# One pace for the weight slabs of a fused attention and gated-FFN layer, with its engine order planned anew

## The chip, the cores and the metric

One core of a Trainium2 chip runs the whole layer. The metric is the device time of one execution in microseconds, as the median of several. Below, PE is TensorE (matmul), ACT is ScalarE, DVE is VectorE, POOL is GpSimd and SP is SyncE, which here issues the DMA transfers.

## The reference

A pre-norm transformer layer over 2048 tokens with model width 1024: 32 query heads of 32 channels that share one key and one value head, then a feed-forward block of width 3584 whose gate is a sigmoid. All tensors are bf16.

```python
def _A_ref(x, wq, wk, wv, wo):
    q = (x @ wq).reshape(B, S, H, Dh).transpose(0, 2, 1, 3)
    k = x @ wk
    v = x @ wv
    p = softmax(einsum("bhqd,bkd->bhqk", q, k) * Dh ** -0.5)
    o = einsum("bhqk,bkd->bhqd", p, v)
    return o.transpose(0, 2, 1, 3).reshape(B, S, H * Dh) @ wo

def _B_ref(x, w_gate, w_up, w_down):
    g = einsum("bsd,df->bsf", x, w_gate)
    u = einsum("bsd,df->bsf", x, w_up)
    return einsum("bsf,fd->bsd", sigmoid(g) * u, w_down)

h = A_x + _A_ref(layernorm(A_x), A_wq, A_wk, A_wv, A_wo)
out = h + _B_ref(layernorm(h), B_w_gate, B_w_up, B_w_down)
```

## The kernel before

**The work.** Tokens are cut into 16 tiles of 128. A tile's attention has two halves of 16 heads each (32 halves in all), and a half is visited once for each of 16 key tiles: 512 visits. A visit is one score group, four matmuls of 512 columns on a quarter of the array's rows each (`S_ps<-QTb,kT`, emitted by `emit_S`), and two exponentials of 128x1024 on ScalarE (L707), which write the probabilities to one of ten slots `Pr` (at first also to four borrowed buffers). VectorE adds the probabilities up (`acc`, L680), so that row sums come from a short matmul over a selector (`F_ps<-acc,sel`, `mk_SUM`); for half 0 they come from matmuls with ones. `mk_PV` multiplies probabilities and values, `mk_OP` is the output projection of a tile (`F_ps<-wo_sb,OT`), `mk_GU` the gate and up matmuls with one tanh for each of 7 groups of 512 channels (L989; the sigmoid is made of a tanh), `mk_D` the down projection (`F_ps<-zone,hact`, 28 matmuls of 512 columns for each half of the width).

**From scores to the next stage.** After the row sums a reciprocal goes through memory to be spread over partitions (`r_scratch`, `rb`, L748 to L751), then OT is scaled (L765), projected, normalized (L871 and the statistics at L349 to L370), and transposed by DMA to `hnT` (`load_hT`), which the gate and up matmuls read.

**Two forms of gate and up.** Mostly the activations are the stationary operand and a weight slab streams, in matmuls of 512 columns (`F_ps<-ring,hnT`); the product then goes through a DMA transpose to `hact`. For the first `ws0` and the last `ws1` tiles the weights are stationary and matmuls of 128 columns give the transposed product at once (`F_ps<-hnT,ring`, four times as many).

**Weight slabs.** Gate and up weights are loaded anew for each tile in slabs of 1024x512, four quarters of 256 KB each (`load_next`), into a ring of four slabs. Once no scores are left, the slots `Pr` hold slabs as well. The two last groups of a pass are the first two of the next, so 40 quarters are loaded a pass. Transfers of slabs and of the down weights are paced: each is held back to the time at which the one before would be through at so many bytes a ns, by a wait on a ScalarE instruction that ends about then (`Plan.step`).

**The order of the work.** Nothing is scheduled on the chip. A planner (`Plan`, and the loop at the end of the kernel) lays out the instruction streams of all engines when the program is built, with costs for each instruction and an expected landing for each transfer. For PE it emits a score group when its inputs are known and ScalarE has less than `run` ns of exponentials in hand, and otherwise a matmul of the current group of another class, chosen by priority lists. Due times place the down groups among the gate and up groups. Copies out of PSUM go to ScalarE or VectorE, whichever the plan finds free first (`evac`), with a handicap for ScalarE of `eb` (keys, values and transposed x) or `eq` (queries). VectorE's additions are held back around the end of a PE group (`hold`). All these are numbers in `TUNE`, so that a change of any of them gives a new order on every engine.

The lines on which the pace hangs:

```python
def fast(self, s):
    return s < 200000.0 or s > self.t_last          # t_last: the plan's time of the last score group
...
if o.pace:
    self.pace_free = s + o.nbytes / TUNE["pace0" if self.fast(s) else "pace"]
```

Of the kernel before, what the change touches and what calls it, by code (L numbers as in the profile page):

```python
# [12 lines left out]
P = 128  # L13
# [2 lines left out]
SEM = 75.0  # L16


TUNE = dict(early=240, look=500, ln_v=1, warm=70, late=300, ws0=1, ws1=1, parts0=3, parts1=4, lord=2, h_ord=2,
            ho=3, ho2=0, pvl1=0, pvl2=0, col_ok=0, pace0=310, swait=400, parts=2, raw=1, rl=0, nd=2, pc=16,  # L20
            rate=315, pace=265, xd=4, qf=1, dall=1, wo_late=1, nkn=3, few=0, rmin=900, hmin=1, h0=100, h1=250,
            hf=1.35, run=700, sum_few=0, pv_few=4, d_off=0, d_a=-1, d_b=1, eb=450, eq=1500)


class Op:
# [16 lines left out]
class Plan:  # L42
# [48 lines left out]

    def fast(self, s):

        return s < 200000.0 or s > self.t_last

    def start_of(self, o):

# [3 lines left out]
        if o.eng == "dve" and o.prio >= 6:  # L101

            for p in self.heap["dve"]:
                if p.prio < 6 and s < p.ready < s + TUNE["look"]:
                    return p.ready
        return s

    def step(self, limit):
# [21 lines left out]
        if o.nbytes:  # L130
            if o.pace:
                self.pace_free = s + o.nbytes / TUNE["pace0" if self.fast(s) else "pace"]
            k = o.key.rstrip("0123456789_")
            go = max(s + 1720.0, self.dma_free)
            w = self.SLOW.get(k, 1.0) if k != "ha" else 2.5 if o.nbytes < 200000 else 1.3
            self.dma_free = go + o.nbytes * w / TUNE["rate"]
            o.end = self.dma_free + 700.0 + self.LATE.get(k, 0.0) + TUNE["late"]
        else:
# [31 lines left out]
def bass_sequential_preLN__grouped_kv_mqa__glu_gated_glu__prompt_kernel(  # L170
# [31 lines left out]
    with ExitStack() as es:  # L202
# [3 lines left out]
        def SB(name, shape, dt=BF16):  # L206
            return EC(nc.sbuf_tensor(name, [P] + shape, dt))
# [12 lines left out]
        r_sb = SB("r_sb", [64], F32)  # L220
# [18 lines left out]
        r_dram = nc.dram_tensor("r_scratch", [32, 64], F32, kind="Internal").ap()  # L239
# [30 lines left out]
        PE, ACT, DVE, POOL, SP = nc.tensor, nc.scalar, nc.vector, nc.gpsimd, nc.sync  # L270

        def dma(fn, key, nbytes, deps=(), prio=5, pace=False, order=(), occ=450.0):
            return pl.op("sp", fn, deps, occ=occ, key=key, nbytes=nbytes, prio=prio, pace=pace, order=order)
# [41 lines left out]

        for c in ["xxqxxqxxxxxxqxxxxq", "qxqxxqxqxxxxxxxxxx", "xqxqxqqxxxxxxxxxxx", "xqxqxqxqxxxxxxxxxx", "xxqxqxqxqxxxxxxxxx"][TUNE["lord"]]:
            if c == "x":
# [19 lines left out]
        def stats(ph, tiles, srcs, deps, prio, after=((), ())):  # L337
# [8 lines left out]
            for t, src, dp in zip(tiles, srcs, deps):  # L346
# [14 lines left out]
                      occ=90, lat=250)  # L361
            if ph and TUNE["ln_v"] or not ph and t0 < 2:

# [80 lines left out]
        def mm(o, l, r, start, stop, **kw):  # L444
            return lambda: PE.matmul(o, lhsT=l, rhs=r, start=start, stop=stop, **kw)  # L445
# [216 lines left out]
        RAW = tuple(range(TUNE["raw"])) + ((NH - 1,) if TUNE["rl"] else ())  # L662
# [20 lines left out]
        def flush_adds(hf):  # L683
            for kt in late_adds.pop(hf, []):
                make_add(hf, kt)
# [42 lines left out]
        rb_ld = {}  # L728
        rs_ev = {}
        rd_ld = {}  # L730
# [3 lines left out]
        def in_row(few):  # L734
            return v_done[0] >= NV or pl.pe_mode == "row" or len(free_slots) <= few or TUNE["col_ok"] and pl.pe_mode == "col"

        def mk_SUM(hf):
            a = acc[:, hf % 2, :]

            def atoms(b):  # L740
                return [(mm(F_ps[DH * j:DH * (j + 1), b, 0:64], sel[:, bb, :], a[:, j * 512 + bb * 64:j * 512 + (bb + 1) * 64],
                            bb == 0, bb == 7, tile_position=(0, DH * j)), 64, "col" if j == 3 else "col-", [])
                        for bb in range(8) for j in range(4)]

            def after(b, last):
                sum_last[hf] = last
                flush_adds(hf + 2)
                rc = pl.op("dve", lambda: DVE.reciprocal(r_sb[:, :], F_ps[:, b, 0:64]),  # L748
                           [last, rd_ld.get(hf - 1)], prio=0, occ=480, lat=560 + SEM)
                rd_ld[hf] = dma(lambda: SP.dma_start(r_dram, r_sb[0:P:4, :]), "rd", 8192, [rc] + (rb_ld[hf - 1] if hf - 1 not in RAW else []), prio=0)  # L750
                rb_ld[hf] = [dma(lambda j=j: SP.dma_start(  # L751
                    rb[DH * j:DH * (j + 1), :], bass.AP(r_dram.tensor, r_dram.offset + 512 * j, [[0, DH], [1, 512]])),
                    "rb", 65536, [rd_ld[hf], ot_ev.get(hf - 1), ot_ev.get(0)], prio=0) for j in range(4)]
                finish(hf)
                return [rc]
            return Group("SUM", atoms, lambda: [add_op.get((hf, NT - 1)), c_sel], after, lambda: in_row(TUNE["sum_few"]))

        def finish(hf):

            if hf not in rb_ld or (hf, len(parts_of(hf)) - 2) not in oun_ev:  # L760
                return
            c, hh = hf // 2, hf % 2
            o = oun[:, hf % 2, :]
            r = rs_b if hf == 1 and hf in RAW else rb[:, :]
            ot_ev[hf] = pl.op("dve", lambda: DVE.tensor_tensor(  # L765
                out=OT[:, 4 * hh:4 * hh + 4, :], in0=o.rearrange("p (a b) -> p a b", a=4),
                in1=r.rearrange("p (a b) -> p a b", a=4), op=ALU.mult),
                [oun_ev[(hf, len(parts_of(hf)) - 2)], op_last.get(c - 1)] + rb_ld[hf], prio=0, occ=600, lat=690)
            if hh == 1:
                for dc in range(2):  # L770
                    queues["OP"].append(mk_OP(c, dc))
# [326 lines left out]
        while True:  # L1098
# [15 lines left out]
            if v < NV:  # L1114
                run = max(pl.free["act"], t) + sum(o.occ for o in pl.heap["act"])
# [187 lines left out]
```

The softmax here doesn't subtract the row's maximum and nothing guards it: scores larger than these inputs give would overflow.

## Time and profile before

The time is 1092.22 us, the median of 3 runs (1091.94 to 1092.35). The profiled execution spans 1092.9 us at a granted PE clock of 0.998.

| engine | busy us | share of the span | instructions |
|---|---|---|---|
| PE, matmul | 1060.6 | 97% | 9314 |
| PE, weight load | 439.3 | 40% | 9454 |
| DVE | 848.9 | 78% | 1054 |
| ACT | 1000.7 | 92% | 1152 |
| POOL | 39.5 | 4% | 61 |

| stretch, us | PE busy | ACT busy | DMA share | GB/s |
|---|---|---|---|---|
| 0 to 50 | 44.05 | 35.48 | 0.83 | 204 |
| 100 to 200 | 96.40 | 98.75 | 0.74 | 227 |
| 500 to 600 | 97.96 | 100.00 | 0.80 | 231 |
| 1000 to 1020 | 19.73 | 10.48 | 1.01 | 299 |
| 1040 to 1060 | 19.32 | 2.39 | 1.04 | 295 |

The page's busy times are averages over three stages with different limits: a start in which the first queries, keys and values are made, a long middle in which scores run, and an end without scores. Matmuls overlap in the array, so a PE that is 97% busy isn't at its peak. In the page's groups of instructions a row gives the line and engine, the output and its inputs, shapes, the number of instructions, their busy time in all, the mean ns of one, and the idle time ahead of them with what ended most of it.

### The profile page before, as it was taken

What the parts mean: (1) busy time and instruction counts of PE and PEld (TensorE: products, weight loads), DVE (VectorE), ACT (ScalarE), POOL (GpSimd) and SP (SyncE); (2) the same over time, 40 slices, a digit from 0 to 9 for tenths busy, and PEclk for the clock granted to TensorE, in tenths of its full rate; (3) what the DMA queues carried; (4) which work ended last, traced back from release to release, by engine and by line L of the source; (5) the groups of instructions that cost most, each with busy time, mean ns of one, the idle gap of its engine ahead of it and who ended that gap; (6) DMA issues with size and microseconds to landing.
All of it is one profiled execution on the core that took longest, in us unless ns stands there. A gap on an engine that the chain in (4) does not pass through costs nothing.

```text
span 1092.9 us, 23470 instructions
## 1 busy us (share of the span) xinstructions
PE 1060.6 (97%) x9314; PEld 439.3 (40%) x9454; DVE 848.9 (78%) x1054; ACT 1000.7 (92%) x1152; POOL 39.5 (4%) x61
## 2 busy tenths in 40 slices
PE   8999999999999999999999999999999999999998
PEld 6533465333333333333333333333333333333485
DVE  8989988787887878787887878787887878787311
ACT  4999999999999999999999999999999999999010
POOL 3300000000000000000000000000000000000000
PEclk9999999999999999999999999999999999999999
DMA  8893399868769595868858595877858586876992
GB/s 248 171 306 121 116 300 279 251 170 269 203 182 266 137 271 144 246 183 255 231 166 256 139 270 147 260 189 229 245 150 262 138 250 168 248 206 194 287 307 95
DMA packets 296509, 233.70 MB, mean 214 GB/s; under 512 B 99536, under 2 KB 282832, under 8 KB 296400
## 3 DMA queue, kind: packets, MB, share of 16 engines
q1 hardware_dynamic: 296400, 232.19, 74.1%
q8 instruction: 75, 1.23, 0.5%
q14 instruction: 34, 0.28, 0.1%
HBM read 203.82 MB, written 8.12 MB: 194 GB/s over the span
## 4 chain that ended last, share of the span: by engine, by line
ACT 67%; PE 22%; issue 5%; DVE 3%; DMA 2%; SPq 0%; DVEq 0%
ACT Pr L707 62%; PE F_ps L445 19%; ACT tnh L989 5%; PE S_ps L445 3%; DVE acc L680 1%; DMA hnT<-hn 1%; DMA r_scratch<-r_sb 1%; DMA zone<-ring 0%; DVE st L349 0%; DVE st L351 0%; DMA ring<-in_A_x_dram 0%; DMA rb<-r_scratch 0%; DVE hact L285 0%; DVE ring L393 0%; DVE OT L765 0%
## 5 line engine op out<-in xcount | busy, mean ns | idle before, releaser
L707 ACT ACTIVATE Pr<-S_ps 128x1024 bf16<-128x1024 f32 x1008 | 956.1, 1181 | 3.4 <-PE S_ps L445 3.4
L680 DVE TENSOR_TENSOR acc<-acc,Pr 128x2048 bf16<-128x2048 bf16 x431 | 524.7, 1217 | 45.4 <-ACT Pr L707 32.1
L445 PE MATMUL F_ps<-ring,hnT 128*128 128x512 bf16 x1506 | 366.8, 380 | 4.4 <-issue 4.1
L445 PE MATMUL F_ps<-zone,hact 128*128 128x512 bf16 x813 | 212.1, 381 | 6.5 <-issue 4.3
L445 PE MATMUL S_ps<-QTb,kT 32*128 32x512 bf16 x2048 | 206.8, 385 | 5.6 <-ACT Pr L707 4.7
L445 PEld LDWEIGHTS F_ps<-ring,hnT 128*128 128x128 bf16 x1536 | 134.6, 98 | 180.8 <-issue 43.0
L989 ACT ACTIVATE tnh<-F_ps 128x512 f32<-128x512 f32 x112 | 83.7, 747 | 60.3 <-PE F_ps L445 60.3
L445 PEld LDWEIGHTS S_ps<-QTb,kT 32*128 32x128 bf16 x2048 | 53.7, 91 | 205.0 <-ACT Pr L707 123.9
L445 PE MATMUL F_ps<-Pr,Vt 128*32 128x512 bf16 x2016 | 134.1, 382 | 0.0
L445 PEld LDWEIGHTS F_ps<-zone,hact 128*128 128x128 bf16 x896 | 75.5, 97 | 104.0 <-issue 34.6
L1010 DVE SCALAR_TENSOR_TENSOR act_s<-tnh,F_ps 128x512 bf16<-128x512 f32 x98 | 67.2, 686 | 58.4 <-PE F_ps L445 58.3
L445 PE MATMUL F_ps<-zone 128*128 128x512 bf16 (+3 forms) x573 | 72.9, 272 | 4.3 <-DVE ring L393 1.0
L445 PEld LDWEIGHTS F_ps<-Pr,Vt 128*32 128x32 bf16 x2016 | 43.0, 95 | 68.0 <-issue 28.6
L445 PE MATMUL F_ps<-wo_sb,OT 128*128 128x512 bf16 x241 | 62.3, 381 | 2.5 <-issue 1.7
L367 POOL TENSOR_TENSOR dsb<-zb,cst 128x1 bf16<-128x1 bf16 x18 | 23.0, 1280 | 964.6 <-DVE zb L364 964.6
L1057 DVE SCALAR_TENSOR_TENSOR h_sb<-F_ps,h_sb 128x512 bf16<-128x512 f32 x32 | 22.1, 692 | 40.4 <-PE F_ps L445 40.3
L445 PEld LDWEIGHTS F_ps<-zone 128*128 128x128 bf16 x584 | 39.0, 97 | 31.3 <-issue 9.2
L680 DVE TENSOR_TENSOR acc<-Pr 128x2048 bf16<-128x2048 bf16 x31 | 37.9, 1224 | 9.7 <-ACT Pr L707 9.7
L445 PE MATMUL F_ps<-hnT,ring 128*128 128x128 bf16 x576 | 37.7, 223 | 0.7 <-ACT tnh L989 0.7
L807 DVE TENSOR_TENSOR oun<-F_ps,oun 128x512 f32<-128x512 f32 x34 | 23.4, 688 | 18.9 <-PE F_ps L445 18.8
L445 PEld LDWEIGHTS F_ps<-hnT,ring 128*128 128x128 bf16 x576 | 33.6, 100 | 6.7 <-issue 5.9
L445 PEld LDWEIGHTS F_ps<-wo_sb,OT 128*128 128x128 bf16 x256 | 21.3, 97 | 34.0 <-issue 12.5
(81 smaller groups left out, 350.9 us busy)
## 6 DMA issues: line engine op xcount, KB each, us to landing
ring<-in_B_w_gate_dram SPq DMA_DIRECT2D x308, 256.0 KB, 3.9
ring<-in_B_w_up_dram SPq DMA_DIRECT2D x308, 256.0 KB, 4.0
rb<-r_scratch SPq DMA_DIRECT2D x124, 64.0 KB, 2.0
zone<-in_B_w_down_dram SPq DMA_DIRECT2D x14, 512.0 KB, 4.5
Pr<-in_B_w_gate_dram SPq DMA_DIRECT2D x20, 256.0 KB, 5.4
Pr<-in_B_w_up_dram SPq DMA_DIRECT2D x20, 256.0 KB, 5.0
ring<-in_A_x_dram SPq DMA_DIRECT2D x16, 256.0 KB, 6.4
h_sb<-in_A_x_dram SPq DMA_DIRECT2D x16, 256.0 KB, 2.9
```

What stands on the lines that cost most here:

```text
L367: g = pl.op("pool", lambda: POOL.tensor_tensor(out=dsb[:, ph, tk], in0=zb[:, ph, tk], in1=half[:, 0:k], op=ALU.pow), [f, c0], prio=0, **sl ...
L445: return lambda: PE.matmul(o, lhsT=l, rhs=r, start=start, stop=stop, **kw)
L680: add_op[(hf, kt)] = pl.op("dve", lambda: DVE.tensor_tensor(out=a, in0=in0, in1=slot, op=ALU.add), dp, prio=6, occ=1135, lat=1255)
L707: exps[u] = pl.op("act", lambda i=i, pb=pb: ACT.activation(out=slot[:, i * 1024:(i + 1) * 1024].rearrange("p (a b) -> p a b", a=2), in_=S_ ...
L807: oun_ev[(hf, part)] = pl.op("dve", lambda: DVE.tensor_tensor(out=o, in0=F_ps[:, b, :], in1=o, op=ALU.add), [last, oun_ev[(hf, part - 1)]] ...
L989: box["a"] = pl.op("act", lambda: ACT.activation(out=tnh[:, :], in_=F_ps[:, b, :], func=ACTF.Tanh, scale=0.5), [last, box.get("e")], prio= ...
L1010: e = pl.op("dve", lambda: DVE.scalar_tensor_tensor(out=so, in0=tnh[:, :], scalar=1.0, in1=F_ps[:, b, :], op0=ALU.add, op1=ALU.mult), [las ...
L1057: e = pl.op("dve", lambda: DVE.scalar_tensor_tensor(out=h_sb[:, t % NHB, sl], in0=F_ps[:, b, 0:DW], scalar=0.5, in1=h_sb[:, t % NHB, sl], ...
```

## The change

`fast` now holds only up to 200 us, since it is also bound to a new number `fast_t`, which is 0. Together with `pace0` (the pace while `fast` holds, 310 to 280) and `pace` (265 to 280) this gives one pace for all slabs: 280 bytes a ns, where there were 310 in the first 200 us and after the last scores, and 265 between. The aim is a supply of weights that keeps the same rate throughout, and a plan that counts on what the transfers deliver.

Along with it the other numbers of the plan were chosen anew: transfers are expected 100 ns later (`late`); the weights are stationary in the last two tiles, not in the last alone (`ws1`); the probabilities of half 1 are multiplied with the values in three parts cut at 5 and 10 (`parts1`); at the start transposed x comes ahead of keys and values and these ahead of queries (`h_ord`), where queries came first; two quarters of a slab must have landed before a gate or up group starts, not three (`nkn`); VectorE's additions are held back only while three probability slots are free, and for longer (`hmin`, `h0`, `h1`); 100 ns more of exponentials may be in hand (`run`); down groups fall due at other places (`d_off`, `d_b`); and ScalarE's handicap for copies is larger for keys, values and transposed x and none for queries (`eb`, `eq`).

One condition in `mk_SUM` (`if hf and ...`) covers half 0, which makes no row-sum store in this setting (`raw=1`).

```diff
-TUNE = dict(early=240, look=500, ln_v=1, warm=70, late=300, ws0=1, ws1=1, parts0=3, parts1=4, lord=2, h_ord=2,
-            ho=3, ho2=0, pvl1=0, pvl2=0, col_ok=0, pace0=310, swait=400, parts=2, raw=1, rl=0, nd=2, pc=16,
-            rate=315, pace=265, xd=4, qf=1, dall=1, wo_late=1, nkn=3, few=0, rmin=900, hmin=1, h0=100, h1=250,
-            hf=1.35, run=700, sum_few=0, pv_few=4, d_off=0, d_a=-1, d_b=1, eb=450, eq=1500)
+TUNE = dict(fast_t=0, early=240, look=500, ln_v=1, warm=70, late=400, ws0=1, ws1=2, parts0=3, parts1=3, lord=2,
+            h_ord=0, ho=3, ho2=0, pvl1=0, pvl2=0, col_ok=0, pace0=280, swait=400, parts=2, raw=1, rl=0, nd=2,
+            pc=16, rate=315, pace=280, xd=4, qf=1, dall=1, wo_late=1, nkn=2, few=0, rmin=900, hmin=3, h0=300,
+            h1=600, hf=1.35, run=800, sum_few=0, pv_few=4, d_off=2, d_a=-1, d_b=-1, eb=700, eq=0)
...
     def fast(self, s):
 
-        return s < 200000.0 or s > self.t_last
+        return s < 200000.0 or s > self.t_last and TUNE["fast_t"]
...
-                rd_ld[hf] = dma(lambda: SP.dma_start(r_dram, r_sb[0:P:4, :]), "rd", 8192, [rc] + (rb_ld[hf - 1] if hf - 1 not in RAW else []), prio=0)
+                rd_ld[hf] = dma(lambda: SP.dma_start(r_dram, r_sb[0:P:4, :]), "rd", 8192, [rc] + (rb_ld[hf - 1] if hf and hf - 1 not in RAW else []), prio=0)
```

## The prediction

> **What bounds the kernel now.** I read the page's chain of waits and its costliest groups first.
>
> ```profile
> ACT 67%; PE 22%; issue 5%; DVE 3%; DMA 2%; SPq 0%; DVEq 0%
> ...
> L707 ACT ACTIVATE Pr<-S_ps 128x1024 bf16<-128x1024 f32 x1008 | 956.1, 1181 | 3.4 <-PE S_ps L445 3.4
> ```
>
> The exponentials on ScalarE (L707) carry two thirds of the path and waited 3.4 us in all. PE carries 22%. To see where one gives way to the other I took the chain in order of time:
>
> ```profile
> 260.14 11.57 ACT Pr L707 x13
> ...
> 322.24 11.57 ACT Pr L707 x13
> ```
>
> The pattern repeats every 62.10 us. In a period lie the scores of one token tile, 64 exponentials and 7 tanhs, with ScalarE busy 100.00 us of each 100 us from 200 to 1000 us. So up to the last exponential nothing but ScalarE's start, its own work and its waits counts. Those I read in the timeline of ScalarE (start, length, what, idle time before it):
>
> ```profile
> 11.56 1.28 ACT L284 ACT_TABLE_LOAD   x1 [11.56 <-DVE kT L285]
> ...
> 14.17 1.94 ACT L707 ACTIVATE Pr<-S_ps 128x1024 bf16<-128x1024 f32 x2 [1.11 <-PE S_ps L445]
> ...
> 17.87 1.94 ACT L707 ACTIVATE Pr<-S_ps 128x1024 bf16<-128x1024 f32 x2 [0.79 <-PE S_ps L445]
> ...
> 24.80 1.02 ACT L707 ACTIVATE Pr<-S_ps 128x1024 bf16<-128x1024 f32 x1 [0.24 <-PE S_ps L445]
> ...
> 148.98 1.02 ACT L707 ACTIVATE Pr<-S_ps 128x1024 bf16<-128x1024 f32 x1 [1.25 <-PE S_ps L445]
> ```
>
> Here are all waits after the first exponential at 14.17: some 1.8 us before 24.80 (with 0.77 ahead of a copy), and one of 1.25 us at 148.98. The last exponential ends at 1009.88. The 1.25 us I looked up in windows of 1 us (columns: length, busy time of PE, PEld, DVE, ACT, POOL, granted PE clock, DMA share, GB/s):
>
> ```profile
> 144.00:145.00 1.00, 0.39 (x2) 0.09 (x2) 1.00 (x2) 1.00 (x3) 0.00 (x0) 1.00 1.13 352
> 145.00:146.00 1.00, 0.96 (x36) 0.65 (x37) 1.00 (x2) 1.00 (x2) 0.00 (x0) 0.72 1.04 335
> 146.00:147.00 1.00, 1.00 (x11) 1.00 (x10) 1.00 (x3) 1.00 (x2) 0.00 (x0) 0.50 1.10 356
> 147.00:148.00 1.00, 1.00 (x13) 1.00 (x11) 0.90 (x2) 0.74 (x1) 0.00 (x0) 0.50 1.09 346
> ```
>
> PE had two score groups in a row with nothing between, stood idle, and got half its clock for about 3 us; 22 weight-held matmuls took 2.5 us instead of 1.2, and the next scores came late. After the last scores PE alone counts (timeline of PE; first and last columns as above, records can be missing):
>
> ```profile
> 1007.59 2.55 PE L445 MATMUL F_ps<-zone,hact 128*128 128x512 bf16 x11
> 1010.06 1.91 PE L445 MATMUL F_ps<-Pr,Vt 128*32 128x512 bf16 x32
> ...
> 1024.71 1.90 PE L445 MATMUL F_ps<-wo_sb,OT 128*128 128x512 bf16 x8 [0.52 <-DVE OT L765]
> ...
> 1040.62 9.09 PE L445 MATMUL F_ps<-hnT,Pr 128*128 128x128 bf16 x160 [1.50 <-DMA hnT<-hn]
> 1049.55 3.74 PE L445 MATMUL F_ps<-hnT,ring 128*128 128x128 bf16 x64
> 1053.34 5.99 PE L445 MATMUL F_ps<-zone,hact 128*128 128x512 bf16 x27
> ...
> 1077.93 12.03 PE L445 MATMUL F_ps<-zone,hact 128*128 128x512 bf16 x54
> ```
>
> PV of the last half starts 0.18 us after the last exponential and PE ends 79.9 us later, with only 0.52 and 1.50 us of named waits, neither on a weight slab. Rates: 160 held matmuls of 128 columns from 1040.62 to 1049.55, 55.8 ns each; those of 512 columns 216 ns (28 from 1053.12 to 1059.17; the first record is missing).
>
> **What the Trainium skill says.** "TensorE: Matmul & The Clock Gate", section "Part 1: The HAM clock gate", says that the array falls to half its clock after an idle window of some 3.4 us; the trace agrees with 0.50 from 146 to 148, though PE there was sparse rather than quite idle. Its section "Wait — 56ns, not 53.3ns?" gives 55.6 and 215.7 ns a matmul, which the 55.8 and 216 confirm. "ScalarE: Activation LUTs", section "What ACT_TABLE_LOAD costs", gives 1283 ns for the load; the trace has 1.28 us.
>
> **The change, part by part.**
>
> The pace itself. A quarter slab has 262,144 bytes: 989 ns at 265 bytes a ns, 936 at 280, 846 at 310. A pass needs 40 of them, 39.6 us before and 37.4 after, in a period of 62.1. Both fit, and ScalarE hides them. At the end 310 was never got: the windows from 1000 to 1060 us show 279 to 299 GB/s at a DMA share near 1, and PE waited for no slab. Going to 280 there costs nothing by itself; in the new order slab n would land about 7.5 + 3.7 us times (n - 8) after the last scores (512 KB halves two by two, 1.05 MB at 280), and the tightest, the last, is due at 68.8 us against 63. Nor does a faster slab stream in the periods touch scores while PE's order keeps its distances: from the row sums to the output projection there are 12.9 us of PE work before and 12.8 after, with 7 score groups between in place of 6.
>
> What counts, then, is the new order. I take it from the order of instructions of the changed kernel.
>
> 1. Start. The new ScalarE order begins with the table load without the wait on kT, and a copy of Q; kT and V of the first tiles go to VectorE. Walked through with the durations of the trace: K and V of tile 0 from 9.46 to 10.13, kT by 10.6 and V by 11.35 on VectorE, transposes of tile 1 at 11.45 (13.17 before), but VectorE evacuates them only at 12.7 to 13.3, behind two statistics of 0.6 each, and the first scores go at 13.65 (13.74 before). First exponential 14.1, against 14.17. The second scores come at 15.3 (17.44), so the first four exponentials run to 17.8 without the 0.8 us and the copy between. Then the fourth weight block of Q, landing at 16.6 in both, holds PE; exponential 4 at 18.9 (19.96). But K of tiles 2 and 3, on ScalarE before, is behind nine instructions on VectorE, to about 24.3, and V's copy on ScalarE waits for it: exponential 8 at 24.85 (24.80). The lead is lost there, and only the copies still to come differ: 2 of Q and 7 before, 1 and 6 after, 2 x 0.27 = 0.54 us. I take -0.5; bounds +0.5 and -2.3 (all waits gone and the copies too).
> 2. The clock dip. No two score groups stand together in the new order. In the same stage it has 0.45 to 1.05 us of other work in each of three gaps of 1.78, sparse but not empty. I take -1.25, bound 0.
> 3. Tanhs. 11 stood behind the last exponential, now 12. One takes 0.48 us of ScalarE (993.49 to 993.97): -0.5.
> 4. The end. From PV on the new order has: PV 1.9 as measured, row sums 0.42, 5 + 16 + 28 + 28 + 28 + 56 = 161 down matmuls and 16 of the projection, 177 x 0.216 = 38.2, and 128 + 64 + 256 + 192 + 96 = 736 held matmuls x 0.0558 = 41.1. Sum 81.6. Before: 1.9 + 0.42, 152 + 16 down and projection plus 64 gate and up, 232 x 0.216 = 50.1, and 448 x 0.0558 = 25.0: 77.4, measured 79.9, so 2.5 of waits and starts. After: the wait for the normalized attention stays, as its chain took 11.2 us from the row sums and the filler is now 16 x 0.216 + 128 x 0.0558 = 10.6: 0.6. The wait for hnT, 11.3 us after the projection, is covered by 64 held, 28 down and 96 held = 15.0: 0. With 0.5 of starts: 82.7. So +2.8; bounds +1.7 (no wait at all) and +4.5 (the chain 1.7 longer). Holding gate and up of the second last tile also costs 448 x 55.8 against 112 x 216 ns, 0.8 us; it is in the sum.
> 5. The remaining edits (three parts for half 1, hold times, due times, landing estimate) move fillers in a stage that ScalarE hides: 0. The condition on the row-sum store touches half 0, which has no such store: 0.
>
> Sum: -0.5 - 1.25 - 0.5 + 2.8 = +0.55, so about 1092.8.
>
> **Rivals.** (a) Faster. The start's lead is kept, since K of tiles 2 and 3 comes earlier than my walk, and the end has no wait: -2.3 - 1.25 - 0.5 + 1.7 = -2.35, 1089.9. For it: the new order has 2.5 us less PE work ahead of score group 17, the planner meant it so. Against: every term must go to its end. (b) Slower. A wait that the periods don't have now: 0.2 us for each of 14 tiles is 2.8, giving 1095.6; or the clock dip stays (1094.1) with the end's chain at its upper bound (1095.8). For it: PE has only some 2% of idle time in a period, and slabs at a faster pace share the one hardware DMA queue with the small transfers of the row sums (5.5 us in the end). Against: no such wait shows in 800 us now, and the new distances are no shorter.
>
> **Numbers.** The central case, within 0.2% (1090.0 to 1094.4): 0.56. Rival (a) 0.12, rival (b) 0.32: more on the slow side, since the gains are bounded and waits are not. The range takes in (a) and most of (b): 1089.8 to 1096.0.
>
> **What would show it.** Step 1: the first and ninth exponentials near 14.1 and 24.9. Step 2: full clock from 130 to 200 us and no wait of ScalarE there. Step 3: the last exponential near 1007.6. Step 4: 82.7 us from there to PE's end, OP waiting some 0.6 us, hnT not at all. It would be wrong if ScalarE waited in the periods, if the half clock came up elsewhere, or if PE waited for slabs at the end.

## The result, and the profile after

The changed kernel takes 1096.0 us (median of 4 runs, 1095.54 to 1096.95), the kernel before on the same chip 1092.08 (1091.56 to 1092.35). The ratio is 1.0038, with a 95% interval of 1.0020 to 1.0055: slower, by 2.2 to 6.0 us. The forecast was 1092.8 (1089.8 to 1096.0), no change to speak of. The time lies at the upper end of that range.

The chain of waits and the row of the exponentials, on the page of the changed kernel:

```profile
PE 63%; ACT 28%; DVE 3%; issue 3%; DMA 2%; SPq 1%; POOL 0%; DVEq 0%
...
L707 ACT ACTIVATE Pr<-S_ps 128x1024 bf16<-128x1024 f32 x1008 | 959.8, 1242 | 0.8 <-PE S_ps L445 0.6
```

The exponentials now wait 0.8 us in all (3.4 before), and the chain has moved from ScalarE to PE. (Waits ahead of ScalarE's copies, here 0.45 and 1.43 us in the start, stand in other rows.) Both look like progress, yet the kernel is slower. The start, in the timeline of ScalarE:

```profile
0.72 1.28 ACT L284 ACT_TABLE_LOAD   x1 [0.72 <-PEq L1288]
...
14.23 3.77 ACT L707 ACTIVATE Pr<-S_ps 128x1024 bf16<-128x1024 f32 x4 [0.63 <-PE S_ps L445]
...
19.05 3.77 ACT L707 ACTIVATE Pr<-S_ps 128x1024 bf16<-128x1024 f32 x4
...
24.91 1.94 ACT L707 ACTIVATE Pr<-S_ps 128x1024 bf16<-128x1024 f32 x2
```

The first, fifth and ninth exponentials are within 0.15 us of the walk in the prediction (14.1, 18.9, 24.85). In windows of 1 us the stage of the clock dip has its full clock:

```profile
146.00:147.00 1.00, 1.00 (x18) 0.67 (x16) 1.00 (x2) 1.00 (x3) 0.00 (x0) 1.00 0.98 295
147.00:148.00 1.00, 0.81 (x10) 0.40 (x8) 1.00 (x3) 1.00 (x3) 0.00 (x0) 1.00 0.87 283
```

The last exponential ends at 1007.5 (forecast 1007.6). The end, in the timeline of PE (the same rows as shown of before):

```profile
1008.22 1.91 PE L445 MATMUL F_ps<-Pr,Vt 128*32 128x512 bf16 x32
...
1022.79 3.40 PE L445 MATMUL F_ps<-wo_sb,OT 128*128 128x512 bf16 x15 [0.42 <-DVE OT L765]
...
1040.30 8.77 PE L445 MATMUL F_ps<-hnT,Pr 128*128 128x128 bf16 x154 [0.30 <-DMA Pr<-in_B_w_up_dram]
...
1079.07 12.03 PE L445 MATMUL F_ps<-zone,hact 128*128 128x512 bf16 x54
```

From PV to PE's end are 82.9 us (forecast 82.7), with 0.42 us for OT (forecast 0.6) and none for hnT. In the changed kernel's second profile, after_again, these are 82.9 us as well, while the last exponential ends at 1008.5. So nearly all that was forecast of the changed kernel came true. What was wrong is the other side of the subtraction. Two more profiles of the kernel before show it.

### The profile page after: what moved, and what is told of

The parts are those of the page before. It is cut to its first block, busy times and chain, and to the rows that moved or that the text cites. A ratio compares the mean times of both kernels' runs of the same rounds, so it can differ in the third digit from the quotient of the medians.

```text
span 1094.1 us, 23956 instructions
## 1 busy us (share of the span) xinstructions
PE 1063.7 (97%) x9653; PEld 459.6 (42%) x9790; DVE 847.9 (78%) x1055; ACT 1000.4 (91%) x1151; POOL 41.2 (4%) x61
## 4 chain that ended last, share of the span: by engine, by line
PE 63%; ACT 28%; DVE 3%; issue 3%; DMA 2%; SPq 1%; POOL 0%; DVEq 0%
PE F_ps L445 52%; ACT Pr L707 25%; PE S_ps L445 11%; ACT tnh L989 2%; DMA ring<-in_A_x_dram 1%; DVE acc L680 1%; DVE st L351 1%; DMA Pr<-in_B_w_up_dram 0%; DMA Pr<-in_B_w_gate_dram 0%; DMA ring<-in_B_w_up_dram 0%; DVE ring L405 0%; SPq L303 0%; DVE st L349 0%; SPq L312 0%; DVE ring L393 0%
## 5 line engine op out<-in xcount | busy, mean ns | idle before, releaser
L445 PE MATMUL F_ps<-ring,hnT 128*128 128x512 bf16 x1404 | 347.2, 380 | 5.5 <-issue 4.1
L445 PE MATMUL S_ps<-QTb,kT 32*128 32x512 bf16 x2048 | 210.5, 385 | 8.2 <-ACT Pr L707 5.3
L445 PE MATMUL F_ps<-zone,hact 128*128 128x512 bf16 x837 | 208.5, 380 | 5.3 <-issue 3.8
L445 PEld LDWEIGHTS F_ps<-ring,hnT 128*128 128x128 bf16 x1456 | 126.4, 98 | 170.1 <-issue 41.2
L989 ACT ACTIVATE tnh<-F_ps 128x512 f32<-128x512 f32 x112 | 88.8, 793 | 63.3 <-PE F_ps L445 63.3
L1010 DVE SCALAR_TENSOR_TENSOR act_s<-tnh,F_ps 128x512 bf16<-128x512 f32 x91 | 62.4, 686 | 39.6 <-PE F_ps L445 38.0
L445 PE MATMUL F_ps<-hnT,ring 128*128 128x128 bf16 x896 | 56.3, 219 | 0.6 <-DMA ring<-in_B_w_up_dram 0.4
L445 PEld LDWEIGHTS F_ps<-hnT,ring 128*128 128x128 bf16 x896 | 50.6, 98 | 7.8 <-issue 5.0
L996 DVE SCALAR_TENSOR_TENSOR hact<-tnh,F_ps 128x512 bf16<-128x512 f32 x21 | 14.4, 685 | 28.4 <-PE F_ps L445 28.4
```

The costliest lines, as they stand in the source:

```text
L989: box["a"] = pl.op("act", lambda: ACT.activation(out=tnh[:, :], in_=F_ps[:, b, :], func=ACTF.Tanh, scale=0.5), [last, box.get("e")], prio= ...
L996: e = pl.op("dve", lambda: DVE.scalar_tensor_tensor(out=ho, in0=tnh[:, :].rearrange("p (f b) -> p f b", b=P), scalar=1.0, in1=F_ps[:, b, : ...
L1010: e = pl.op("dve", lambda: DVE.scalar_tensor_tensor(out=so, in0=tnh[:, :], scalar=1.0, in1=F_ps[:, b, :], op0=ALU.add, op1=ALU.mult), [las ...
```

## Experiments

Every kernel below computes the whole layer. "Counted work" is the sum over PE's instructions in their order, with 216 ns for a full matmul of 512 columns, 55.8 ns for a held one of 128, and a quarter of 216 for one that uses a quarter of the array. Time minus counted work is PE's lost time: its waits, half clock, and what else the count leaves out.

### The kernel before, again, and the changed one again

No edit (`before_again`, `before_third`, `after_again`).

> The kernel before once more, unchanged, for a second profile. Theory (the execution profiled first was slow for itself: it took 1094.73 us where the median is 1092.1): the new profile has no half clock near 145 us, ScalarE ends its last exponential near 1007.3 to 1008.6 in place of 1009.9, and the span is near 1090.3. Rival (the profiled execution is typical and the time is lost in the kernel after): half clock and the wait of 1.25 us again, last exponential at 1009.9, span near 1092.9. Ratio 1.000 in both.

> The kernel before once more, for a third profile. Theory (the transfers of 6.6 us for hnT and 5.5 us for the row sums in the end of the first profile were slow ones): hnT in 3.9 to 4.5 us, the row sums' store in 3.5 to 4.3, no wait of PE on either, 77.5 to 78.5 us from PV of the last half to the end of PE. Rival (they are usual): the waits of 0.5 and 1.5 us again, 79.9 us.

> The kernel after, unchanged, beside the runs below. Theory: last scores near 1004.6, end of PE near 1091, 1.0038 times before.

Measured: before_again 1091.85 us (ratio 0.9996, 0.9988 to 1.0004), before_third 1092.39 (one execution), after_again 1096.17 (ratio 1.0032, 1.0020 to 1.0044). The end of the kernel before in before_again, PE's timeline:

```profile
1010.32 1.91 PE L445 MATMUL F_ps<-Pr,Vt 128*32 128x512 bf16 x32
...
1024.28 1.89 PE L445 MATMUL F_ps<-wo_sb,OT 128*128 128x512 bf16 x8
...
1038.52 9.10 PE L445 MATMUL F_ps<-hnT,Pr 128*128 128x128 bf16 x160
...
1076.03 12.03 PE L445 MATMUL F_ps<-zone,hact 128*128 128x512 bf16 x54
```

No wait for OT and none for hnT: 77.7 us from PV to PE's end, and 77.6 in before_third, where the prediction had read 79.9. The issues of transfers in the end tell why (size and us to landing); first the profile that the prediction was made from, then before_again:

```profile
r_scratch<-r_sb SPq DMA_DIRECT2D x1, 8.0 KB, 5.5
hnT<-hn SPq DMA_TRANSPOSE x1, 6.6
```

```profile
r_scratch<-r_sb SPq DMA_DIRECT2D x1, 8.0 KB, 4.2
hnT<-hn SPq DMA_TRANSPOSE x1, 3.9
```

Two small transfers beside the slab stream landed 1.3 and 2.7 us later in the first profile, and PE waited 0.52 and 1.50 us for what came of them. That execution took 1094.73 us, 2.5 over the median of its kernel. Of the 78 executions of the kernel before that ran beside the experiments four took over 1094 us. Its waits are no part of a usual execution (before_third has none either, with its transpose for hnT landing after 4.9 us, later than I had expected), but the prediction subtracted them from a median that doesn't hold them.

The clock dip is there again in both, so the theory of before_again was wrong in that point. Of the 78 executions the mean clock was 0.998 in 42 (the value of the three profiles with the dip) and 1.000 in 36; their medians are 1092.86 and 1091.82. So executions with the dip take 1.0 us more, and it comes in about half of them; the changed kernel was at 1.000 in all 9.

What of PE's idle time? The page's first part lists busy time and number of instructions by engine. The changed kernel in its first profile:

```profile
PE 1063.7 (97%) x9653; PEld 459.6 (42%) x9790; DVE 847.9 (78%) x1055; ACT 1000.4 (91%) x1151; POOL 41.2 (4%) x61
```

and in after_again:

```profile
PE 1080.4 (99%) x9790; PEld 458.5 (42%) x9790; DVE 847.5 (77%) x1055; ACT 1000.6 (91%) x1151; POOL 41.3 (4%) x61
```

One program, once with 137 matmul records fewer than weight loads and once with all of them: the idle 2% are the missing records. With all records PE is busy 100.00 us of each 100 from 200 to 1000, as ScalarE is. ("Perfetto Trace Analysis" in the Trainium skill, section "Tensor Engine Instruction (MATMUL, LD_WEIGHTS)", says that the end of a matmul record is an estimate; the records here average 0.38 us where the matmuls follow at 0.216. So busy time alone doesn't show that PE is full, but no wait is between them.)

The three profiles of the kernel before lack 140 records each; before_no_double (below), the same order but for ten matmuls, has all of them and the same 100.00. The chain of waits hangs on this too. It gave ScalarE 67% in the kernel before; the page of before_no_double has

```profile
PE 94%; ACT 2%; DVE 2%; DMA 1%; issue 0%; SPq 0%; DVEq 0%
```

and the changed kernel's chain is 63% PE in its first profile and 85% in after_again. The seven profiles with all records give PE 70 to 94% of the chain, the ten others 22 to 63%. So the 67% from which the prediction started doesn't show that ScalarE alone sets the time.

PE's lost time by stage then says where the 4 us are:

| us | counted work | lost to score group 33 | from there to 512 | after it | PE's end |
|---|---|---|---|---|---|
| before_again | 939.2 | 17.9 | 129.9 | 1.0 | 1088.1 |
| before_third | 939.2 | 18.2 | 129.4 | 0.8 | 1087.6 |
| changed, first profile | 940.1 | 19.8 | 129.0 | 2.2 | 1091.1 |
| after_again | 940.1 | 20.4 | 129.3 | 2.2 | 1092.1 |

By the means of the pairs: +2.05 us lost in the start, -0.5 in the middle, +1.3 in the end, and 0.9 more work (the second held tile): +3.75, against 3.9 between the medians. In the end, 0.5 of the 1.3 is that PV starts 0.69 us after the last exponential, where it was 0.16 to 0.18. The start, where the prediction saw a small gain, is the largest term. PE's windows of before_again (length, busy PE with count, clock, DMA share, GB/s):

```profile
13.00:20.00 7.00, 6.06 (x96) 1.00 1.08 368
20.00:30.00 10.00, 10.00 (x129) 1.00 0.52 136
30.00:48.00 18.00, 17.11 (x230) 1.00 0.83 149
```

and of after_again:

```profile
13.00:20.00 7.00, 5.41 (x87) 1.00 1.09 362
20.00:30.00 10.00, 9.13 (x121) 1.00 0.53 145
30.00:48.00 18.00, 15.83 (x205) 1.00 0.77 137
```

PE does 2.8 us less between 13 and 48 us in this pair (1.9 from before_third to the changed kernel's first profile), though ScalarE gets its first scores as early. Its longest wait there is 1.46 us for a block of wq (0.76 in before_again). Two others, in the timeline of PE of after_again:

```profile
21.80 3.23 PE L445 MATMUL F_ps<-zone 128*128 128x128 bf16 x56 [0.85 <-DVE zone L285]
...
34.23 1.48 PE L445 MATMUL F_ps<-zone 128*128 128x256 bf16 x12 [0.67 <-DVE Vt L285]
```

Both are for copies on VectorE (L285). The new handicaps didn't put them there: the four copies of transposed x (`zone`) and this copy of V ran on VectorE in before_again too, and PE had no such wait. They start later now, the one for `zone` at 21.06 us in place of 20.19, that of V at 33.99 in place of 31.10. Score groups went on, so the exponentials hardly waited; the work that PE didn't do went to the end of the kernel.

### The dip alone

In before, ten gate and up matmuls are moved from behind two adjoining score groups to between them:

```diff
+        pe = pl.lists["pe"]
+        i = next(i for i in range(400, 3000) if all(o.tag is None for o in pe[i:i + 8]))
+        j = next(j for j in range(i + 8, i + 80) if pe[j].tag == "GU")
...
+        pe[i + 4:j + 10] = pe[j:j + 10] + pe[i + 4:j]
```

> The kernel before with ten gate matmuls moved from behind to between the two score groups that stand together near 144 us; nothing else. Theory (those two leave PE idle, and in some executions it then gets half its clock near 146 us, which costs up to 1.25 us): no half clock, ScalarE without a wait near 148 us, 0.3 to 1.0 us less than before. Rival (the half clock's loss is made up by the end): within 0.3 us.

Measured: 1091.76 us, ratio 0.9994 (0.9985 to 1.0002). All 13 executions ran at a clock of 1.000; the median is that of the kernel before without a dip (1091.82). So the two adjoining groups make the dip, and step 2's gain is 1 us in every second execution, half a microsecond in the median. The interval takes in 1, so the time of this run alone shows neither the theory nor its rival. In its profile the last exponential ends at 1008.4 and PE takes 78.3 us from PV on.

### The pace by its three places

In before, with all other numbers kept (of the changed line, the number is shown). `first_pass_280` and `mid_pace_280`:

```diff
-pace0=310
+pace0=280
```

```diff
-rate=315, pace=265
+rate=315, pace=280
```

`end_pace_only` keeps 265 after the last scores, and `pace_280_everywhere` has all three at 280:

```diff
-        return s < 200000.0 or s > self.t_last
+        return s < 200000.0 or False
```

> The kernel before with 280 bytes a ns in place of 310 in the first 200 us alone. By the count of the order PE then has 86.9 us of work after the last scores in place of 79.5, and no two score groups stand together. Theory (what PE hasn't done by the last scores is done after them, and ScalarE sets when those are): 5 to 7 us slower, 1097 to 1099.5. Rival (the early pace is hidden behind ScalarE, as the middle's is): within 1 us of before.

> The kernel before with 280 instead of 265 bytes a ns between 200 us and the last scores, 310 at both ends. Counted work left after the last scores 79.3 us, as before (79.5). Theory: with the same work left and ScalarE hiding the middle, the time is that of the kernel before within 2 us, 1091 to 1094, and the last scores come at 1005 to 1008. Rival: a faster pace in the middle collides with the small transfers of the row sums, ScalarE waits in the periods, last scores 1009 or later and 1095 to 1100.

> The kernel before with the pace after the last scores at the middle's 265 in place of 310; the order moves by a single matmul in the end. Theory (pace is not what sets the end; PE's remaining work is): within 0.3 us of before. Rival (slabs at a lower pace come late at the end): 14 slabs of 1.05 MB at 265 in place of 290 to 310 bytes a ns are 4 to 8 us more of transfer, so PE would wait and the time be 2 to 4 us longer, with PE waiting for slabs after 1010 us.

> The kernel before with the pace of the change alone: 280 bytes a ns from first to last, all other numbers of the plan as they were. Counted from its order of instructions, PE has 84.5 us of work left after the last scores, 79.5 in the kernel before and 84.3 in the changed one. Theory: the early pace decides how much PE has done by the last scores, and what is left sets the end. So at least as slow as the changed kernel, 1096 to 1111, the upper value if the last scores also come late (near 1013), as with 280 in the first 200 us alone. Rival, the prediction's own step: the pace costs nothing and the new order is all, 1091 to 1093.

| edit of before | us | ratio (95%) | lost to group 33 | to 512 | after |
|---|---|---|---|---|---|
| 280 to 200 us | 1110.36 | 1.0156 (1.0137 to 1.0176) | 18.8 | 142.3 | 5.3 |
| 280 in the middle | 1094.10 | 1.0015 (1.0007 to 1.0024) | 18.3 | 128.6 | 2.3 |
| 265 at the end | 1097.10 | 1.0042 (1.0031 to 1.0054) | 18.0 | 129.1 | 5.3 |
| 280 throughout | 1116.09 | 1.0207 (1.0186 to 1.0229) | 18.6 | 142.5 | 11.2 |

My expectation for the first (5 to 7 us) was a third of what came, and the last came 5 us over its own. Going to 280 "costs nothing by itself" is plainly wrong in the old order: it costs 22.6 us (2.07%), and the three places alone add up to 2.13%. The expensive place is the beginning. PE's timeline of pace_280_everywhere near 216 us:

```profile
215.60 0.60 PE L445 MATMUL F_ps<-ring,hnT 128*128 128x512 bf16 x2 [1.51 <-DMA ring<-in_B_w_up_dram]
216.13 0.40 PE L445 MATMUL S_ps<-QTb,kT 32*128 32x512 bf16 x4
217.97 1.02 PE L445 MATMUL F_ps<-ring,hnT 128*128 128x512 bf16 x3 [1.44 <-DMA ring<-in_B_w_gate_dram]
```

and its windows of 1 us after that:

```profile
218.00:219.00 1.00, 1.00 (x7) 0.25 (x7) 0.90 (x2) 0.50 (x1) 0.00 (x0) 0.72 0.93 280
219.00:220.00 1.00, 1.00 (x6) 0.29 (x7) 0.90 (x2) 0.44 (x1) 0.00 (x0) 0.50 0.60 198
220.00:221.00 1.00, 1.00 (x4) 0.32 (x3) 0.72 (x1) 1.00 (x2) 0.00 (x0) 0.50 0.76 221
```

Two waits for slabs, 2.95 us, stand ahead of score groups in PE's order. PE is busy 0.40, 0.53 and 0.03 us of the three us before 218 and has half its clock for most of the next 4, and ScalarE then waits 1.06 and 0.53 us for scores. From score group 102 to 106 PE loses 7.1 us, where before_again loses 1.0. That is half of the 12.6 us that it loses more between groups 33 and 512; the rest comes in small steps that I didn't trace to a cause. 37.4 us of transfers do fit in a period of 62.1, as "The pace itself" has it; but in these lines one late slab stops PE, with the score groups behind it in its order. In the end the same kernel waits four times for slabs, 7.1 us in all; the three longest:

```profile
1050.10 1.46 PE L445 MATMUL F_ps<-Pr,hnT 128*128 128x512 bf16 x6 [1.49 <-DMA Pr<-in_B_w_gate_dram]
1052.76 0.61 PE L445 MATMUL F_ps<-Pr,hnT 128*128 128x512 bf16 x2 [1.21 <-DMA Pr<-in_B_w_gate_dram]
1056.18 3.57 PE L445 MATMUL F_ps<-Pr,hnT 128*128 128x512 bf16 x8 [2.81 <-DMA Pr<-in_B_w_up_dram]
```

In end_pace_only the rival was right too: PE waited 0.72 and 0.89 us for slabs near 1037 and 0.73 and 1.22 near 1075. I read the first two as the work of the queue. SyncE's timeline of end_pace_only:

```profile
1025.99 0.47 SPq L946 DMA_DIRECT2D Pr<-in_B_w_up_dram  x1
1031.78 0.36 SPq L1064 DMA_DIRECT2D out_dram<-h_sb  x1
1032.19 2.22 SPq L946 DMA_DIRECT2D Pr<-in_B_w_up_dram  x2
```

The store of an output (L1064) waited 5.4 us for VectorE, and the slab issues planned behind it stood still with it; the load fell to 205 GB/s from 1030 to 1040. In before_again 13 quarters of slabs were issued from 1022.44 to 1028.77, ahead of the store. So here the slower pace in the plan moved issues behind a store that waits.

The middle behaved nearly as the theory had it: 1.7 us slower, 0.1 over the expected range.

### The other numbers, from both sides

In before, `two_held_only` (`ws1=2`) and `before_new_start` (`h_ord=0, eb=700, eq=0, parts1=3`); in the changed kernel, `after_one_held` (`ws1=1`), `after_fast_end`, `after_first_pass_310` (`pace0=310`; as `fast` holds up to 200 us only, this is the early pace alone) and `after_old_start` (`h_ord=2, eb=450, eq=1500, parts1=4`). after_fast_end:

```diff
-                self.pace_free = s + o.nbytes / TUNE["pace0" if self.fast(s) else "pace"]
+                self.pace_free = s + o.nbytes / (310 if s > self.t_last else TUNE["pace"])
```

`before_then_after` takes before's numbers up to score group 464 and the changed kernel's from there (`LATER` holds all that the change sets):

```diff
+            if v == 464:
+                TUNE.update(LATER)
```

> The kernel before with weights stationary in the last two tiles (ws1=2), nothing else. PE has 80.2 us of work after the last scores in place of 79.5 (counts of the order times 216, 55.8 ns). Theory (the end is the sum of PE's work): +0.7 us, 1092.8. Rival (the two held tiles are what costs the 4 us, by waits of their own): +2 us or more.

> The kernel before with the start of after alone: h_ord=0, eb=700, eq=0, parts1=3. The count gives 84.5 us of work left after the last scores, 79.5 before. Theory (ScalarE starts a little sooner, but PE does 2 us less by 48 us, since it waits for copies on VectorE, and does it at the end): last scores 1 to 2 us sooner, the end 5 us longer, 3 to 5 us slower. Rival (the start only gives ScalarE's lead): 0.5 to 1 us faster.

> The kernel after with weights stationary in the last tile alone (ws1=1). PE has 83.2 us of work after the last scores, where the kernel after has 84.3 and the kernel before 79.5. Theory (sum of PE's work): 1.1 us less than after, near 1094.9, so still some 2.8 slower than before. Rival (two held tiles cost the 4 us): near before, 1092.

> The kernel after with 310 bytes a ns once no scores are left; 280 before that, as in after. Work left after the last scores is the same 84.3 us, its order differs a little. Theory (after's order has room for its slabs; what costs is that 84.3 us are left where before has 79.5): within 0.7 us of after. Rival (slabs at 280 come late at the end, as they did at 265 in the order of before, which cost 4.6 us): 2 to 4 us less than after, near before.

> The kernel after with 310 bytes a ns in the first 200 us in place of 280. The count gives 95.1 us left after the last scores in place of 84.3. Theory (work left sets the end, whatever the pace is called): last scores within 1.5 us of after's, 9 to 12 us slower than after, 1105 to 1108. Rival (310 is the better early pace, as 280 cost before 17.8 us): faster than after.

> The changed kernel with the old numbers of the start (queries ahead of keys and values, the old handicaps of ScalarE for copies, half 1 in four parts). Counted work left after the last scores 84.3 us, as in the changed kernel, though PE has 2.3 us more done by score group 20. Theory: the start isn't what costs; last scores 1004 to 1007, PE's end some 86 us later, 1095 to 1098. Rival: the new start is what makes the changed kernel slower, and without it 1092 to 1094.

> Numbers and order of the kernel before up to score group 464 (some 910 us), the numbers of the kernel after from there on. By the count PE has 83.1 us left after the last scores. Theory (what is left after the last scores sets the time): last scores near 1004.5 as PE has done 2.7 us less by then, end 1 to 3 us later than before. Rival (all of the loss is from the start): within 0.7 us of before.

| run | us | ratio to before (95%) | lost to group 33 | to 512 | after |
|---|---|---|---|---|---|
| two_held_only | 1095.22 | 1.0025 (1.0015 to 1.0035) | 18.3 | 128.2 | 3.4 |
| before_new_start | 1108.61 | 1.0153 (1.0136 to 1.0170) | 20.7 | 139.4 | 4.1 |
| after_one_held | 1098.51 | 1.0054 (1.0042 to 1.0066) | 19.9 | 129.0 | 4.1 |
| after_fast_end | 1097.20 | 1.0042 (1.0030 to 1.0055) | 20.0 | 129.4 | 2.8 |
| after_first_pass_310 | 1108.37 | 1.0152 (1.0137 to 1.0168) | 20.0 | 140.5 | 3.0 |
| after_old_start | 1097.77 | 1.0052 (1.0037 to 1.0067) | 21.2 | 130.9 | 1.2 |
| before_then_after | 1101.73 | 1.0092 (1.0076 to 1.0107) | 18.0 | 129.8 | 8.6 |

What follows:

- The fast pace after the last scores isn't what the changed kernel lacks: after_fast_end isn't better than the changed kernel (1.0042 against 1.0032 to 1.0038), and on the same chip its median is 1.0 us over after_again's.
- The second held tile costs 2.7 us in before, more than its work (0.85 us): PE waited 1.97 us for `hact` (L996) ahead of the projection. But taking it out of the changed kernel doesn't help; the plan then has slab waits of 0.67, 0.53 and 0.39 us. My expectations, +0.7 and -1.1, counted work and no waits.
- The loss in the start goes with the start's numbers: put into before they give 20.7 to group 33 where it has 18.0. Taken out of the changed kernel, PE has lost as little as before by score group 17 (13.5 against 15.5 in the changed kernel's first profile), but then waits once, in the timeline of PE of after_old_start,

```profile
56.86 1.44 PE L445 MATMUL F_ps<-zone 128*128 128x256 bf16 x24 [2.14 <-DMA zone<-ring]
```

and the gain is gone by group 33 (21.2). Its expectation (1095 to 1098, the start isn't what costs) held in the number. I read it more narrowly: this start brings no gain to this plan, because another wait takes its place.
- before_new_start came 12 us over its expectation. Part of this its profile shows. Two score groups stand together in its order from 166 to 170 us, with a single other matmul ahead of them, and half the clock follows (windows of 1 us):

```profile
169.00:170.00 1.00, 0.47 (x6) 0.13 (x10) 0.99 (x3) 1.00 (x2) 0.00 (x0) 1.00 0.98 325
170.00:171.00 1.00, 1.00 (x16) 0.34 (x8) 1.00 (x1) 1.00 (x2) 0.00 (x0) 0.50 1.04 352
```

From score group 77 to 87 PE loses 7.1 us there, in before_again 3.7.
- An early pace of 310 costs the changed order some 13 us (1.0152 against 1.0032), an early pace of 280 the old one 17 (1.0156). So neither pace is the better one by itself: the early pace and the other numbers belong together. before_then_after came 7 us over the upper end of its expectation, with slab waits of 1.50 and 1.62 us in the end. That a plan joined from two has its slabs at times that suit neither is my reading; the waits are less than half of the 7.6 us that it loses more than before_again after the last scores.

No version beat the kernel before by more than its interval.

## Why the prediction was wrong

**Step 4, the end, is what failed in the sum**, in its side of before. The prediction set 82.7 against 79.9; the changed kernel had 82.9, the kernel before, in two other profiles, 77.7 and 77.6. So the term is +5.2, not +2.8. The prediction's own count of that side, 77.4, was near; it set its count for the new kernel against a measurement for the old one. The 79.9 came from the profile of an execution 2.5 us over the median, with 2.0 us of waits for late transfers of its own. The prediction saw both waits and took them for the kernel's. Its upper bound, +4.5, was too low as well, since it let only the changed kernel vary.

**Steps 1 to 3, the last exponential.** The number came true in the first pair of profiles: forecast -2.25, measured 1009.9 to 1007.5. In the repeats it is 1010.2 and 1009.9 to 1008.5. Most of it is the dip: against before_no_double, which has none, the changed kernel's two profiles gain 0.9 us and nothing, where steps 1 and 3 promised 1.0. And the premise that "up to the last exponential nothing but ScalarE's start, its own work and its waits counts" is half the truth. PE is just as full, and what it hasn't done by then it does afterwards. The last scores came 2.0 us earlier (1007.5 to 1005.5, in the two repeats) and PE had 4.8 us more counted work behind them (84.3 against 79.5): 0.9 of it is added work, the rest is moved. Rival (a) even counted 2.5 us less PE work ahead of score group 17 in favour of a faster kernel; by the table above such work is the largest part of the loss. The "some 2% of idle time" of PE were missing records, and where a profile has them, as that of before_no_double, the chain goes to PE.

**Step 2, the dip.** The mechanism was right. Its size was 1.0 us where there is a dip, in about half of the executions, so some 0.5 in the median and not 1.25.

**The pace itself.** Costed at nothing by the share of a period that transfers take. In the old order it costs 22.6 us, and with the other numbers of the change some 18.5 of these are won back (ratio 1.0207 to 1.0038). For the changed order as a whole the statement held: no wait for a slab over 0.66 us in its two profiles. But the reason given for it, that the transfers fit in a period, holds in the old order as well, where they came late.

**Step 5**, the edits at nothing: the middle lost 0.5 us less than before, so nothing shows there against it.

**Rivals.** The time is that of (b), 1095.6 with an interval around it, but by none of its ways: ScalarE didn't wait in the periods (0.8 us in all), the dip went, and the end's chain wasn't longer (0.42 us). That its number fits is chance.

**What stays open.** Which of the changed numbers keeps the early slabs in time at 280 was not separated: the runs show that the early pace has to match the rest of the plan, not which number does it. Of the 10 us that before_new_start loses more than before between score groups 33 and 512, some 3 go with its half clock; the rest was not traced. That the start's numbers slow PE in the start is shown by putting them into before (20.7 against 18.0); which of them does it, the order or the handicaps, is not shown. Nor did taking out any of four parts of the change make the changed kernel faster: the table of lost time says where the 4 us lie, but no run shows a changed kernel without them.

## What to carry to other kernels

When two engines are full side by side, an earlier end of one is no gain by itself: add up the other's work and lost time over the whole span, for work that isn't done early is done late. Subtract like from like: before a difference of two profiles is added to a median, see how far the profiled execution is from that median, and don't take its waits on small transfers for the kernel's own. Compare the numbers of matmul and weight load records before reading PE's idle time or the chain. A pace that suffices on average says nothing of a single slab in a fixed order; cost a changed pace by the due time of each slab, the first ones too.

## What the runs showed of the hardware

- After two PE waits of 1.51 and 1.44 us, with little work between, the clock was 0.72, 0.50, 0.50 and 0.58 in the four us from 218, and even a PE that was sparsely busy got half its clock (at 146 us, in about half of the executions of one program). It didn't always come: in the profile of first_pass_280 PE was busy 1.96 us of the 4 from 216 on, with a wait of 1.52, and the clock stayed at 1.00. The Trainium skill, "TensorE: Matmul & The Clock Gate", section "Part 1: The HAM clock gate", speaks of an idle window of some 3.4 us after which the clock is halved, and says that the window runs freely, so that the number of slow matmuls at a kernel's start varies between runs. The variation between executions here, in mid-kernel, agrees, and 3.4 us of full idleness weren't needed (the longest wait ahead of a half clock was 1.51 us).
- Over all profiles the transpose by DMA for the last hnT landed after 3.3 to 7.0 us, and the store of 8 KB for the last row sums after 3.1 to 5.5, beside the slab stream.
- In end_pace_only nothing passed a store that waited 5.4 us at the head of SyncE's queue: the loads behind it were issued only after it, at 1032.19.
